# One written order for the whole program, and a written place for every temporary

## The chip, the cores and the metric

The kernel runs on one core of a Trainium2 chip. The metric is the device time of one execution in microseconds. Five engines matter: TensorE (PE, matrix products), VectorE (DVE), ScalarE (ACT), GpSimd (POOL), and SyncE (SP), which here only issues transfers between the chip's large memory (HBM) and the working memory (SBUF). Products are summed in PSUM, which has eight banks of 512 float32 per partition.

## What is computed

Attention in which each of 8 batches and 8 heads has 512 local tokens and 32 global ones, followed by a gated two-layer network over all 4608 tokens:

```python
s_g   = scale * q_g @ concat(k_g, k_l).T          # global queries see all keys
out_g = softmax(s_g) @ concat(v_g, v_l)
s_ll  = where(abs(i - j) <= 32, scale * q_l @ k_l.T, -1e9)
s_l   = concat(scale * q_l @ k_g.T, s_ll)         # local ones: a window and the globals
out_l = softmax(s_l) @ concat(v_g, v_l)

x   = concat(out_g, out_l) as (4608 tokens, 512)
xn  = x / sqrt(mean(x * x) + 1e-6) * rms_g
g   = xn @ w_gate                                 # 512 x 1536
h   = g * sigmoid(g) * (xn @ w_val)
out = h @ w_out                                   # 1536 x 512
```

## The kernel before

**Chunks.** The work is cut into nine chunks. Chunks 0 to 7 are the 512 local tokens of one batch each; chunk 8 is the 256 global tokens. While the network of chunk c runs on PE, the local attention of chunk c+1 and the global attention of some batch are threaded between its products. Attention is in float32. The network is in float16: every operand is split into a high and a low part, and each product is three products of parts. Chunks 0 and 1 do both layers plainly; chunk 2 does the first layer with seven block products in place of eight (tiles pq), chunks 3 to 7 do so for both layers (pq and pr), chunk 8 for the second.

**Steps.** The functions of the kernel are cut into named steps. In chunk 0: L, V and W load q and k, v, and a slice of weights; S (scores), M (mask and minimum), E (exponent), T (transposes), C (copies), A (products with v), R, X, Q, Z (division, sums of squares) are a unit of attention; m, s, k or l, g, q, p, e, a, d turn one weight slice into its two parts (a makes the high part on ACT, d the low one on DVE); N, D, U, H, Y are the norm; I are the first layer's products, B, b, h, c, r the gate on ACT and DVE (c a cast on ACT, r a subtraction on DVE, which give the two parts of h); O are the second layer's products; J, j, u, w build the sums of weights that the block products need and store them to HBM (wd, wa, wb). So r4 is r for slice 4, and M7.1 is M of unit 7, half 1. In chunks 1 to 8 a step has its chunk in front: P and O are products, R what follows a product, t the gate's tail, n the next chunk's norm, w the weight loads and folds due at that point, and a name with a slash (GT/1+1) is a step of an attention unit of a later chunk. From chunk 2 on the weights come back from HBM: `fetch` (L1339) loads a tile wt for two block products, `fetch_out` (L1348) a tile wu, all on SP's queue.

**Order.** All engines run under a manual schedule (L1903): each engine's queue holds its instructions in the order in which the program calls them, and every dependence between engines becomes a semaphore wait. For chunk 0 the order is the list ORDER, run step by step at L1904. For chunks 1 to 8 the steps are first recorded by `write` (L1910), cut where the engine changes, and then called in the order of one list per chunk at L2038:

```python
for c, plan in plans.items():
    for name in orders.get(c, plan):
        for call in plan.pop(name) if c in orders else plan[name]:
            call()
```

So all steps recorded under chunk c stand ahead of all those under chunk c+1, on every engine. L1929 in the profile is the helper that records, and so the line of nearly all instructions of chunks 1 to 8.

**Places.** A temporary takes the next buffer of its pool in rotation and waits until that buffer's earlier content is released. The pools in SBUF: wf 12 buffers of 4 KB a partition (weights, wt, wu, u, v, results), wo 7, h 6, st 6 of 4.5 KB, v 4, x 2, q 2, k 2, e 4, w 3, t 3, xh and xl 4 each, gpt 1. In PSUM: pa has four banks (attention), po two, pg one and pv one (products). Every PE product that begins a new sum, and every load, takes its buffer this way.

Of the kernel before, what the change touches and what calls it, by code (L numbers as in the profile page):

```python
# [39 lines left out]
ORDER = """  # L40

# [22 lines left out]


_ORDER_1 = """
w0.0 S/0+1.0 M1/0+1.0 E1/0+1.0 w2.0 M3/0+1.0 E3/0+1.0 P0.0 N2/0+1.0 P1.0 N3/0+1.0 M2/0+1.0 E2/0+1.0
N1/0+1.0 M0/0+1.0 w3.0 w5.0 E0/0+1.0 N0/0+1.0 F0/0+1.0 P4.0 w6.0 F3/0+1.0 P5.0 R5.0 R6.0 P8.0 P9.0
F1/0+1.0 D1/0+1.0 R9.0 R1.0 F2/0+1.0 D3/0+1.0 D3/0+1.1 R10.0 P6.0 P7.0 R7.0 D0/0+1.0 D2/0+1.0
D2/0+1.1 R2.0 T2/0+1.0 P10.0 P11.0 w8.0 w9.0 P12.0 P2.0 T3/0+1.0 P3.0 D0/0+1.1 T0/0+1.0 D1/0+1.1  # L70
T1/0+1.0 A/0+1.0 B/0+1.0 P14.0 w12.0 Y/0+1.0 R3.0 R4.0 R5.1 w14.0 R11.0 R12.0 w1.0 X/0+1.0 R8.0 R9.1
GL/1+1.0 w15.0 P18.0 P16.0 P17.0 X/0+1.1 P19.0 Y/0+1.1 R17.0 R18.0 R19.0 R20.0 P13.0 R13.0 P32.0
P33.0 w18.0 GS/1+1.0 GM/1+1.0 Y/0+1.2 R13.1 GN/1+1.0 P24.0 P25.0 R14.0 w45.0 w20.0 w21.0 GM/1+1.1
GN/1+1.1 GT/1+1.0 GN/1+1.2 GT/1+1.2 GT/1+1.1 GT/1+1.3 P15.0 R15.0 L/2+1.0 S/2+1.0 R33.0 R34.0
M0/2+1.0 M2/2+1.0 N0/2+1.0 w49.1 N1/2+1.0 M3/2+1.0 N3/2+1.0 w24.0 E3/2+1.0 F3/2+1.0 P20.0 w17.0
R21.1 P40.0 D3/2+1.0 R25.0 R26.0 N2/2+1.0 R16.0 E2/2+1.0 R17.1 P21.0 R21.0 P22.0 P23.0 D3/2+1.1
R22.0 R23.0 T3/2+1.0 w26.0 w27.0 R24.0 R25.1 P26.0 P27.0 R27.0 R28.0 V/2+1.0 E0/2+1.0 F0/2+1.0
M1/2+1.0 F2/2+1.0 P28.0 P29.0 P41.0 R41.0 R29.1 X/0+1.2 w30.0 Y/0+1.3 P34.0 w23.0 P35.0 P30.0
D0/2+1.0 D0/2+1.1 R29.0 P31.0 R35.0 w44.0 P42.0 R30.0 R31.0 GV/1+1.0 R42.0 E1/2+1.0 GA/1+1.0 P43.0
F1/2+1.0 D1/2+1.0 D1/2+1.1 T1/2+1.0 w32.0 w33.0 L/0+2.0 R36.0 R37.1 P36.0 GD/1+1.0 P38.0 P66.0 R43.0  # L80
R44.0 D2/2+1.0 T0/2+1.0 D2/2+1.1 T2/2+1.0 w38.0 P37.0 R37.0 R38.0 w47.0 R45.1 w40.0 A/2+1.0 B/2+1.0
Y/2+1.1 X/2+1.0 X/2+1.1 w41.0 R32.0 P39.0 X/2+1.2 P44.0 P45.0 Y/2+1.0 X/2+1.3 Y/2+1.2 Y/2+1.3 R39.0
R40.0 R45.0 R46.0 R41.1 S/0+2.0 N0/0+2.0 M3/0+2.0 n53.0 P46.0 P47.0 n53.1 w46.0 R47.0 E3/0+2.0 n55.0
n55.1 n55.2 N1/0+2.0 n55.3 V/0+2.0 N2/0+2.0 n55.4 w48.0 n55.5 R33.1 N3/0+2.0 M2/0+2.0 E2/0+2.0
F2/0+2.0 P48.0 P67.0 P68.0 P49.0 P50.0 n55.6 n55.7 n55.8 n55.9 n55.10 w48.1 w35.0 P69.0 P70.0 n55.11
n55.12 n55.13 P51.0 P52.0 n56.0 R48.0 R49.0 P71.0 D2/0+2.0 M1/0+2.0 w46.1 n57.0 GX/1+1.0 w29.0
M0/0+2.0 D2/0+2.1 E0/0+2.0 n57.1 n64.1 w42.0 w49.0 w51.0 n65.0 P53.0 F3/0+2.0 n63.2 R71.0 w11.0
R53.0 F0/0+2.0 P54.0 P55.0 w54.0 w43.0 E1/0+2.0 F1/0+2.0 n56.1 n58.0 n58.1 R71.1 n62.1 n59.0 n59.2
P56.0 P57.0 D0/0+2.0 D0/0+2.1 n61.1 w56.0 P58.0 P59.0 n59.1 n63.0 P60.0 P61.0 GX/1+1.1 T2/0+2.0
w57.0 R53.1 D3/0+2.0 D3/0+2.1 D1/0+2.0 D1/0+2.1 T1/0+2.0 n64.0 n63.1 n60.0 n61.0 n65.1 T3/0+2.0  # L90
P62.0 P63.0 w59.0 P64.0 P65.0 R65.0 T0/0+2.0 R59.0 n62.0 R65.1 R59.1 n66.0
"""
# [187 lines left out]
def attention_moe_kernel(  # L280
# [363 lines left out]
    def local_unit(c, hp):  # L644
# [1523 lines left out]
```

## Time and profile before

| | |
|---|---|
| three runs | 917.7, 919.26, 921.77 us (median 919.26) |
| profiled execution | span 922.7 us from first to last instruction; no other time of it is given |
| busy | PE 878.8 us (95%), DVE 724.5, ACT 556.3, POOL 273.2 |
| mean granted TensorE clock | 0.980 |
| read from HBM, written | 183.2 MB, 27.0 MB |
| DMA packets' share of the 16 engines' span | 69.5% for the hardware queue that carries the loads |

Busy time is the union of an engine's instructions. PE's matmuls are pipelined and their ends are modelled, so a busy PE may still lose short waits. The granted clock is a share of 2.4 GHz: 0.50 is the lower of the two levels, 1.2 GHz.

### The profile page before, as it was taken

The page shows a single profiled execution, that of the slowest core. Times are in us where ns is not written, and L with a number is a line of the kernel's source. Part 1 is how long each engine was busy: PE and PEld are TensorE (multiplying, and loading weights), DVE is VectorE, ACT ScalarE, POOL GpSimd, SP SyncE. Part 2 cuts the span into 40 slices and gives each one's busy share as a digit, 9 for nine tenths or more (in the row PEclk, how much of TensorE's full clock was granted, in tenths as well). Part 3 has the DMA queues.
Part 4 walks back from the last instruction along what each step waited for, and adds up shares of the span by engine and source line. Part 5 has one row for each costly group of instructions (what it writes and reads, how often), then busy time and mean ns, then how long its engine had stood idle before and what let it go on. Part 6 is the DMA issues. An engine that isn't in the chain of part 4 may idle for free.

```text
span 922.7 us, 27756 instructions
## 1 busy us (share of the span) xinstructions
PE 878.8 (95%) x11430; PEld 671.4 (73%) x11430; DVE 724.5 (79%) x1831; ACT 556.3 (60%) x1341; POOL 273.2 (30%) x244
## 2 busy tenths in 40 slices
PE   5699989999999999999999999898999999999998
PEld 4644445544547886588888888787888888888887
DVE  6899998868796887877987888587887897777554
ACT  6899995636452755457565767466575862456132
POOL 0000000032435776306440244122520454133311
PEclk9699989999999999999999999999999999999999
DMA  9983615495377869686677769667876666888665
GB/s 337 405 301 106 192 47 173 130 333 174 90 248 243 274 206 300 194 257 233 206 258 263 245 222 293 198 208 243 265 250 223 206 222 244 247 246 273 215 232 191
DMA packets 101006, 212.03 MB, mean 230 GB/s; under 512 B 8080, under 2 KB 34448, under 8 KB 100880
## 3 DMA queue, kind: packets, MB, share of 16 engines
q1 hardware_dynamic: 100448, 209.94, 69.5%
q8 instruction: 89, 1.46, 0.6%
q10 hardware_dynamic: 432, 0.33, 0.1%
q14 instruction: 37, 0.30, 0.1%
HBM read 183.24 MB, written 27.00 MB: 228 GB/s over the span
## 4 chain that ended last, share of the span: by engine, by line
PE 40%; DVE 5%; DMA 3%; ACT 3%; issue 2%; POOL 1%; DVEq 0%; ACTq 0%; POOLq 0%; SPq 0%
PE pq L1929 20%; PE pr L1929 14%; PE p L1929 3%; DMA wt<-wd 2%; ACT e L1929 1%; PE a L1929 1%; DVE v L1929 1%; DMA wu<-wb 1%; DVE s L1929 1%; DVE u L1929 1%; POOL hs L1929 1%; POOL hu L1929 1%; PE s L1929 1%; ACT s L1929 1%; DVE t L1929 1%
## 5 line engine op out<-in xcount | busy, mean ns | idle before, releaser
L1929 PEld LDWEIGHTS <-wt 128*128 128x128 f16 x3312 | 322.7, 98 | 56.9 <-issue 11.1
L1929 PE MATMUL pq<-xh,wt 128*128 128x256 f16 x1152 | 206.6, 274 | 6.8 <-DMA wt<-wd 2.5
L1929 PE MATMUL pq<-ht,wt 128*128 128x256 f16 x1296 | 158.0, 274 | 2.1 <-POOL ht L1929 1.2
L1929 PE MATMUL pq<-xl,wt 128*128 128x256 f16 x576 | 157.8, 274 | 0.1
L1929 ACT ACTIVATE e<-e,sm 128x128 f32<-128x128 f32 x288 | 104.2, 390 | 27.8 <-DVE sm L1929 27.8
L1929 POOL TENSOR_TENSOR hu<-v,hu 128x256 f16<-128x256 f32 (+1 forms) x60 | 56.5, 958 | 177.6 <-ACT hu L1929 155.1
L1929 PE MATMUL pr<-wu,hs 128*128 128x256 f16 x792 | 92.4, 273 | 0.3 <-DVE hs L1929 0.3
L1929 POOL TENSOR_TENSOR e<-e,sm 128x512 f32<-128x512 f32 x24 | 27.7, 1162 | 205.3 <-DVE sm L1929 205.3
L1929 PEld LDWEIGHTS <-hs 128*128 128x128 f16 x792 | 77.4, 98 | 9.7 <-DVE hs L1929 0.6
L1929 POOL TENSOR_TENSOR hs<-u,hs 128x512 f16<-128x512 f32 x50 | 60.5, 1228 | 65.6 <-ACT hs L1929 37.9
L1929 PE MATMUL pr<-wu,hu 128*128 128x256 f16 x594 | 70.8, 273 | 1.0 <-DMA wu<-wb 0.6
L1929 DVE TENSOR_TENSOR s<-pq,s 128x512 f32<-128x512 f32 x66 | 44.9, 685 | 29.9 <-PE pq L1929 14.1
L1929 ACT ACTIVATE t<-u,half_inv 128x512 f32<-128x512 f32 x72 | 49.6, 717 | 27.0 <-DVE u L1929 23.0
L1929 DVE SCALAR_TENSOR_TENSOR t<-t,u 128x512 f32<-128x512 f32 x72 | 54.0, 758 | 14.4 <-ACT t L1929 14.3
L1929 ACT COPY s<-pq 128x512 f32<-128x512 f32 x72 | 41.3, 580 | 38.3 <-DVE s L1929 18.2
L1929 PEld LDWEIGHTS <-hu 128*128 128x128 f16 x594 | 57.6, 98 | 8.6 <-DMA wu<-wb 0.9
L1929 DVE TENSOR_TENSOR v<-pq,s 128x512 f32<-128x512 f32 x72 | 49.0, 683 | 18.6 <-PE pq L1929 14.8
L1929 PE MATMUL po<-wo,h 128*128 128x512 f16 x288 | 63.4, 379 | 0.0
L1651 PE MATMUL p<-xh,wf 128*128 128x512 f16 x192 | 58.8, 379 | 3.1 <-DVE t L1763 1.2
L1929 PE MATMUL p<-xh,wf 128*128 128x512 f16 x192 | 59.8, 385 | 0.5 <-DVE t L1929 0.5
L1651 PEld LDWEIGHTS <-wf 128*128 128x128 f16 x288 | 27.7, 98 | 37.0 <-issue 3.1
L1929 PEld LDWEIGHTS <-wf 128*128 128x128 f16 x288 | 27.8, 99 | 34.6 <-issue 2.9
(380 smaller groups left out, 1704.7 us busy)
## 6 DMA issues: line engine op xcount, KB each, us to landing
wt<-wd SPq DMA_DIRECT2D x120, 512.0 KB, 5.3
wu<-wb SPq DMA_DIRECT2D x36, 512.0 KB, 5.3
wr<-in_w_in_dram SPq DMA_DIRECT2D x24, 512.0 KB, 8.7
wu<-wa SPq DMA_DIRECT2D x24, 512.0 KB, 4.7
k<-in_qkb_dram SPq DMA_DIRECT2D x24, 448.0 KB, 6.5
gkq<-in_gkq_dram SPq DMA_DIRECT2D x16, 576.0 KB, 7.1
wt<-wd SPq DMA_DIRECT2D x36, 256.0 KB, 4.2
v<-in_vb_dram SPq DMA_DIRECT2D x24, 352.0 KB, 5.6
```

The costliest lines, as they stand in the source:

```text
L1651: nc.tensor.matmul(ps[:, :n], rows[:, a, o : o + P], ch[z][k][:, :n], start=(k == 0 and i == 0), stop=(k == NK - 1 and i == 2),)
L1929: return lambda *a, **k: write(self.engine, lambda: call(*a, **k))
```

## The change

1. ORDER and the eight lists per chunk are replaced by one list ORDER of all 3365 pieces, each with its chunk in front; a list JOBS, equal to the old ORDER, only says in which order chunk 0's steps are recorded. The set of pieces is the same; chunk 0's steps are now cut where the engine changes, too, so that the parts of a step can stand apart, and pieces of neighbouring chunks may mix.
2. The pools are gone. SBUF holds 43 pages of 4 KB a partition and 8 wide ones of 4.5 KB, and the lists PAGES and BANKS give, in the order of recording, the page (with the quarter at which it begins) or the bank of each temporary. Temporaries under 1 KB a partition get memory of their own. All eight PSUM banks serve every use.
3. The transposed exponents of global attention are two tiles instead of one, and loads of gv and k are placed by their own size. A scratch space for DMA descriptors is set to 2048 bytes.

No instruction, shape, queue or engine changes. The core of the diff:

```diff
-ORDER = """
-
+JOBS = """
...
+NPAGE, NWIDE = 43, 8
+
+ORDER = """
+0:L0.0 0:S0.0 0:L1.0 0:L3.0 0:M0.0.0 0:M0.1.0 0:L2.0 0:W0.0 0:V0.0 0:S1.0 0:W1.0 0:M1.0.0 0:E0.0.0
...
+0:Y0.1.0 0:d1.0 0:q2.0 0:q3.0 0:S4.0 0:H0.0.0 0:d0.0 0:Y0.0.0 0:M4.0.0 0:U0.3.0 0:m5.0 0:H0.3.0
+0:U0.2.0 0:m4.0 0:I1.10.0 0:H0.2.0 0:k5.0 0:I0.00.0 0:Y0.3.0 0:s5.0 0:M4.1.0 0:Y0.2.0 0:k4.0 0:p2.0
...
+0:d12.0 0:S7.0 0:T5.0.0 0:C5.1.0 0:B11.0 0:O0.0.0 0:c6.0 0:M7.0.0 0:b11.0 0:C5.0.0 0:c4.0 0:A5.0
+0:a13.0 0:c7.0 0:R5.0 0:M7.1.0 0:a14.0 0:d13.0 0:Q4.0 0:O0.1.0 0:O0.2.0 0:M6.0.0 0:c5.0 0:a17.0
+0:a15.0 0:r6.0 0:r5.0 0:O1.1.0 0:V6.0 0:r7.0 0:O1.0.0 0:h11.0 0:E7.0.0 0:E7.1.0 0:O0.3.0 0:O1.3.0
...
+    page = [con.tile([P, 1024], F32, tag=f"page{i}", name=f"page{i}") for i in range(NPAGE)]
+    wide = [con.tile([P, 1152], F32, tag=f"wide{i}", name=f"wide{i}") for i in range(NWIDE)]
+    banks = [psum.tile([P, 512], F32, tag=f"bank{i}", name=f"bank{i}") for i in range(8)]
+    page_at, bank_at, smalls = iter(PAGES.split()), iter(BANKS.split()), [0]
+
+    def tile_of(shape, dt, name):
+        n = int(np.prod(shape[1:])) * (2 if dt in (F16, BF16) else 4) // 4
+        if n < 256:
+            smalls[0] += 1
+            tag = f"{name}_{smalls[0]}"
+            return con.tile(shape, dt, tag=tag, name=tag)
+        at = next(page_at)
+        if n > 1024:
+            t = wide[int(at[1:])][:, :n]
+        else:
+            of, i = (wide, at[1:-1]) if at[0] == "W" else (page, at[:-1])
+            q = ord(at[-1]) - ord("a")
+            t = of[int(i)][:, q * 256 : q * 256 + n]
...
+    def bank_of(name):
+        return banks[int(next(bank_at))]
...
     def fetch(c, g, i):
-        t = pool.tile([P, 2, 2, 2, HT], F16, tag="wf", bufs=NF, name=f"wt{c}_{g}{i}")
+        t = tile_of([P, 2, 2, 2, HT], F16, f"wt{c}_{g}{i}")
...
-    for c, plan in plans.items():
-        for name in orders.get(c, plan):
-            for call in plan.pop(name) if c in orders else plan[name]:
-                call()
-        assert c not in orders or not plan
+    for name in ORDER.split() or list(plan):
+        for call in plan.pop(name):
+            call()
+    assert not plan
```

In the old ORDER the same place of chunk 0 reads `a12 T5.0 d12 O0.0 O0.1 c8 Q4`, with c4 to c7, r4 to r7 and all M steps of units 4 to 7 ahead of it. In the old lists a load stands among the steps of its own chunk or the end of the chunk before; in the new one some stand a chunk earlier, as 3:w22.0 between steps of chunks 1 and 2.

## Rows read from the trace of the kernel before

**Rows 1.** The page, its first part: TensorE's busy time, its share of the span and its instructions; then PE's weight loads and the other engines.

```profile
PE 878.8 (95%) x11430; PEld 671.4 (73%) x11430; DVE 724.5 (79%) x1831; ACT 556.3 (60%) x1341; POOL 273.2 (30%) x244
```

**Rows 2.** Busy time by stage, core 0: the stretch (us from the start), its length, the busy time of PE, PE's weight loads, DVE, ACT and POOL with their counts, the granted share of TensorE's full clock, the mean busy share of the DMA engines, GB/s.

```profile
0.00:46.00 46.00, 29.16 (x611) 24.46 (x612) 34.42 (x151) 35.70 (x104) 0.20 (x4) 0.78 0.98 371
46.00:130.00 84.00, 76.37 (x712) 38.90 (x710) 81.23 (x193) 80.20 (x139) 0.00 (x0) 0.97 0.53 178
130.00:172.00 42.00, 42.00 (x496) 23.67 (x497) 35.69 (x84) 26.29 (x66) 0.00 (x0) 0.98 0.32 108
172.00:286.00 114.00, 110.67 (x1184) 55.09 (x1165) 90.80 (x241) 56.59 (x168) 40.83 (x32) 0.99 0.68 210
286.00:387.00 101.00, 100.16 (x1477) 74.12 (x1477) 80.31 (x195) 55.79 (x145) 61.81 (x45) 1.00 0.77 246
387.00:489.00 102.00, 98.49 (x1505) 85.78 (x1495) 81.59 (x208) 61.80 (x159) 38.04 (x35) 1.00 0.76 242
489.00:589.00 100.00, 95.92 (x1456) 84.00 (x1454) 80.08 (x207) 65.78 (x174) 31.53 (x30) 1.00 0.76 244
589.00:690.00 101.00, 98.15 (x1449) 84.88 (x1447) 77.15 (x201) 65.21 (x172) 32.23 (x29) 0.97 0.73 239
690.00:873.00 183.00, 182.37 (x2179) 160.21 (x2177) 139.29 (x293) 95.15 (x192) 61.29 (x58) 1.00 0.73 235
873.00:922.60 49.60, 45.55 (x416) 40.32 (x414) 23.91 (x65) 13.78 (x27) 7.25 (x13) 1.00 0.61 213
```

**Rows 3.** The list of waits, PE alone, from 0 to 172 us: who waited, for whom, us in total, times, the longest.

```profile
...
PE x00t L1110 <- DVE dg L1104: 6.3, 1, 6.3
...
PE t L732 <- ACT e L717: 4.1, 2, 3.0
...
```

**Rows 4.** The same list from 172 us to the end, whole. "issue" is time in which the engine waited for nothing that the profile shows.

```profile
PE pq L1929 <- DMA wt<-wd: 3.4, 4, 2.2
PE gt L1929 <- ACT ge L1929: 2.6, 2, 2.3
PE a L1929 <- issue: 2.4, 2, 2.2
PE pq L1929 <- DVE s L1929: 1.9, 4, 1.2
PE pq L1929 <- ACT u L1929: 1.5, 1, 1.5
PE pq L1929 <- POOL ht L1929: 1.2, 1, 1.2
PE pq L1929 <- DVE u L1929: 0.6, 1, 0.6
PE pr L1929 <- DMA wu<-wb: 0.6, 1, 0.6
PE p L1929 <- DVE t L1929: 0.5, 1, 0.5
PE pr L1929 <- DVE oo L1929: 0.4, 1, 0.4
PE pr L1929 <- DVE hs L1929: 0.3, 1, 0.3
```

**Rows 5.** Busy time by stretch again, for the three stretches after 172 us in which the granted clock was halved (columns as in rows 2).

```profile
210.50:213.90 3.40, 3.40 (x34) 1.43 (x39) 0.86 (x3) 1.54 (x4) 0.00 (x0) 0.50 0.57 160
589.40:592.80 3.40, 3.40 (x18) 2.36 (x17) 0.30 (x1) 1.32 (x4) 0.00 (x0) 0.50 0.99 266
626.90:630.30 3.40, 3.16 (x15) 2.24 (x16) 0.31 (x1) 3.35 (x14) 0.51 (x1) 0.50 0.99 295
```

**Rows 6.** The chain of waits, from 495 to 510 and from 615 to 650 us: start, length in us, what the chain ran through.

```profile
498.07 9.17 PE pq L1929 x84
...
623.53 3.56 DMA wt<-wd
...
639.43 4.27 DMA wt<-wd
```

**Rows 7.** The waits of SyncE's queue, which issues the transfers, over the whole run (columns as in rows 3), and the issue row of the page for the larger wt loads: count, KB each, median us from issue to landing.

```profile
SPq L1929 <- PE pq L1929: 142.3, 65, 9.9
...
SPq L1929 <- PE a L1929: 34.4, 4, 27.2
...
wt<-wd SPq DMA_DIRECT2D x120, 512.0 KB, 5.3
```

**Rows 8.** Groups of chunk 0. The first row is from the view of one line (L1794, chunk 0's output products): durations min/median/max in ns, first and last start in us. The others are groups from 0 to 172 us, with shapes kept apart: busy us, mean ns of one, idle time before.

```profile
L1794 PE MATMUL po<-wo,h x144: 379/379/634, 129.1 to 170.1; 128*128 128x512 f16 x144
...
L702 DVE CUSTOM_DVE_ANT_0 e<-s,mask 128x128 f32<-128x128 f32 x64 | 14.2, 291 | 8.6 <-PE s L688 8.6
...
L369 DVE TENSOR_TENSOR h<-t,h 128x512 f16<-128x512 f32 x12 | 8.1, 687 | 0.0
...
L485 ACT ACTIVATE wr<-wr 128x512 int16<-128x512 int16 x22 | 27.4, 1378 | 0.9 <-DVE w3t L474 0.9
...
L1774 ACT CAST h<-t 128x512 f16<-128x512 f32 x12 | 7.0, 610 | 0.3 <-DVE t L1766 0.3
```

**Rows 9.** The views of tile t on DVE and of tile h on POOL: durations min/median/max in ns, first and last start.

```profile
L1929 DVE SCALAR_TENSOR_TENSOR t<-t,u x72: 650/685/1625, 298.3 to 847.8; 128x512 f32<-128x512 f32 x72
...
L1929 POOL TENSOR_TENSOR h<-t,h x23: 1151/1164/2016, 193.6 to 360.9; 128x512 f16<-128x512 f32 x23
```

More of the change, by code (lines that the diff above doesn't have):

```diff
@@ L72 @@
[L72 to L77, printed above, removed]
@@ new lines @@
+8:R16.2 8:R8.4 8:R8.0 8:R16.4 8:P19.0 8:P30.0 8:P37.0 8:P16.0 8:P46.0 8:P32.0 8:R8.1 8:P33.0 7:R59.0
+8:R8.2 8:R8.3 8:R9.1 8:P17.0 8:w4.0 8:P31.0 8:R33.0 8:R10.0 8:R10.2 7:O36.0 8:P28.0 8:P29.0 7:O37.0
+8:R17.0 8:R18.4 7:O38.0 8:R10.3 8:R37.0 8:P22.0 8:R29.0 8:P47.0 8:R19.0 8:w42.0 8:R34.4 8:R18.0
+8:P34.0 8:R24.1 8:R30.0 8:R18.1 8:P24.0 8:O0.0 8:P23.0 8:P25.0 8:R23.0 8:R24.4 8:R24.0 8:R24.2
+8:R25.0 7:t45.2 8:R38.0 8:O3.0 8:R31.0 8:P38.0 8:R24.3 8:R16.3 8:R26.4 8:R17.1 8:R18.2 8:w32.0
+8:P35.0 8:R25.1 8:P39.0 8:R39.0 8:P26.0 8:R35.0 8:P27.0 8:R26.0 8:P42.0 8:R27.0 8:w44.0 8:P44.0
@@ new lines @@
+8:R10.1 8:O31.0 8:O24.0 8:O25.0 8:O26.0 8:O32.0 8:R34.1 8:R34.3 8:O27.0 8:O28.0 8:R56.2 7:R62.1
+8:O29.0 8:O33.0 8:O34.0 8:R62.0 8:R26.1 8:O35.0 8:R50.1 8:R65.0 8:R65.1 8:O36.0 8:O37.0 8:O38.0
+8:O39.0 8:O40.0 8:O41.0 8:R68.0 8:R68.1
+"""
+PAGES = """
+3a 0a 1a 0a 1a 0c 2a 0c 1c 7a 8a 22a 0a 5a 6a 5a 9a 10a 5c 0a 3c 4a 6a 20c 3c 2a 11a 7a 12a 13a 14a
+15a 3c 4a 16a 5a 1a 17a 6a 3c 18a 19a 15a 3c 23a 24a 9a 10a 16a 20c 14a 18c 7a 4a 20c 6a 15a 0a 3c
+20c 20b 20a 3d 0b 20a 21a 20d 21a 23a 9a 2a 8a 12a 13a 17a 28a 29a 26a 27a 30a 41a 24a 19a 22a 24c
@@ L679, in scores @@
             q, k = st["q"], st["k"]
-            st["sm"] = pool.tile([P, 3, 8], F32, tag="sm", bufs=SMB, name=f"sm{u}")
-            ps = st["ps"] = [bank(f"s{u}{h}", "pa") for h in range(2)]
+            st["sm"] = tile_of([P, 3, 8], F32, f"sm{u}")
+            ps = st["ps"] = [bank_of(f"s{u}{h}") for h in range(2)]
             for i in range(NT):
@@ L794, in load @@
             if w == 0:
-                late["mask"] = con.tile([P, 6 * P], F32, tag="mask", name="maskb")
+                late["mask"] = tile_of([P, 6 * P], F32, "maskb")
                 nc.sync.dma_start(late["mask"], maskb)
@@ L885, in scores @@
             st["et"] = [
-                pool.tile([P, 1088], F32, tag="k", name=f"et{u}{x}") for x in range(2)
+                tile_of([P, 1088], F32, f"et{u}{x}") for x in range(2)
             ]
@@ L909, in values @@
             if ms[0] == blocks[0]:
-                st["a"] = [attn_bank(f"a{u}{p}") for p in range(4)]
+                st["a"] = [bank_of(f"a{u}{p}") for p in range(4)]
             ps = st["a"]
@@ L931, in values, with taken @@
                         )
-        def take(z):
+        def taken(z):
             x = x_part(c, 2 * hp + z)
@@ L1362, in moe_pair @@
         st = {}
-        bank = {6: "po", 1: "pg", 5: "pv"}
+        own = (6, 1, 5)
         onto = {7: 6, 4: 6, 3: 5, 2: 1}
@@ L1374, in products @@
             hi, lo = ch["op"][p]
-            first = p in bank
+            first = p in own
             for j in range(2):
@@ L1903, in attention_moe_kernel @@
     ctx.enter_context(tc.manual_schedule(engines=every))
-    for name in ORDER.split():
-        job.pop(name)()
-    plans = {c: {} for c in range(1, NCH)}
-    at_work = [1, "", 0, ""]
+    plan = {}
+    at_work = [0, "", 0, ""]
     now = nc
@@ L1911, in write @@
         c, step, n, on = at_work
-        if on and (on != engine or step[0] in "Rtn"):
+        if on and (on != engine or c and step[0] in "Rtn"):
             n += 1
         at_work[2:] = n, engine
-        name = f"{step}.{n}"
-        assert name not in plans[c] or name == next(reversed(plans[c])), name
-        plans[c].setdefault(name, []).append(call)
+        name = f"{c}:{step}.{n}"
+        assert name not in plan or name == next(reversed(plan)), name
+        plan.setdefault(name, []).append(call)
     def doing(c, step):
@@ L1936, in attention_moe_kernel @@
     nc = Written
+    for name in JOBS.split():
+        doing(0, name)
+        job.pop(name)()
     stores = [steps[3] for f, steps in folds.items() if f"J{f}" not in job]
```

768 lines of the change are left out of this document (427 added, 341 removed), and 9 rows, old and new, of the table BANKS.

## Prediction

> **What bounds the kernel now.** I read the page's busy row first [rows 1]. TensorE (PE) is busy 878.8 of 922.7 us, so 43.9 us is all that any order of the same steps can take out of its idle time; VectorE (DVE) at 724.5 and ScalarE (ACT) at 556.3 look far from a limit, but these are means over stages that differ. So the second view is busy time by stage, cut where chunks begin [rows 2]. From 0 to 46 us PE is idle for 16.8 us; from 46 to 130 us for 7.6 us, while DVE is busy 81.2 of 84 and ACT 80.2 of 84: there both are the bound, and PE waits for what they make. From 130 to 172 us PE is never idle. After 172 us its idle time is 3.3, 0.8, 3.5, 4.1, 2.9, 0.6 and 4.1 us a stage, 19.3 in all, of which some 3.5 is the last result going out. The two chunks from 690 to 873 us lose 0.6 together: a chunk can run nearly without loss when its inputs come in time.
>
> The third view is the list of waits. Before 172 us PE waits longest for the norm of chunk 0 (dg, 6.3 us) and for attention exponents [rows 3]. After it [rows 4] I split the list by whom PE waits for: 4.0 us for transfers (wt 3.4, wu 0.6), and 11.4 us for DVE, ACT, POOL and an unnamed releaser: 2.6 + 2.4 + 1.9 + 1.5 + 1.2 + 0.6 + 0.5 + 0.4 + 0.3. The clock adds to these: three stretches of 3.4 us ran at 1.2 GHz, a granted clock of 0.50 [rows 5], each at or just after one of the three waits of 2.2 us or more of rows 4; work done there would take half as long at 2.4 GHz, so each costs 1.7 us. The fourth view is the chain of waits: at 623.5 us it leaves PE and runs through a load of wt for 3.56 us, at 639.4 us again for 4.27 [rows 6]. These loads were issued late because SyncE (SP) was held: it waited 142.3 us in 65 waits for PE to finish with a buffer that a load was to overwrite, and once 27.2 us for attention [rows 7]. A transfer of 512 KB takes 5.3 us to land [rows 7], and SP's queue is in order, so loads behind the held one wait too.
>
> **The change, part by part.** No arithmetic, transfer or instruction is dropped; every term is one of position. I compare positions thus: a 12-matmul P step costs PE 84 matmuls in 9.17 us, 109 ns each, 1.31 us [rows 6], and the work of an engine that stands ahead of a step in its queue is the sum of its steps in the order.
>
> *Chunk 0.* The point that sets PE's lateness is O0.0, chunk 0's first output product, which began at 129.1 us [rows 8] and behind which PE has 42 us without idle time. Its weights come last from d12 on DVE. Both orders put the same PE work ahead of O0.0. Ahead of d12 the new one leaves out r4 to r7, four 128x512 subtractions of 687 ns, and M7.1 and one M6 step, two times four mask operations of 291 ns with their reads hidden in part: 14.2 us over 64 is 0.22 us each, 1.8 for eight [rows 8]. 2.7 + 1.8 = 4.5 us less on the engine that is busy 97% of this stage. If ACT held O0.0 instead, the four casts c4 to c7 of 610 ns that go behind it make 2.4 at most [rows 8]. What is put off comes after, beside 42 us in which DVE is busy 35.7 and ACT 26.3 [rows 2]; 4.5 more leaves DVE 1.8 free: the cover is thin, and if it is gone, r4 to r7 make the O steps of chunk 0 late by what is over. The new order also puts k5 and parts of chunk 1's attention (S4, M4.0) ahead of chunk 0's first product: k5 is two ACT operations, 2.5 us [rows 8], which makes that product later at first. So the bounds are +2.5 and -7.6 (all idle time of this stage), and I take -4.5, from the rows of the engine that makes O0.0's last input.
>
> *Transfers.* I count, for each of the 222 loads of wt and wu, the PE work that the written order has between the load and the first P or O step that reads it. Before: half have less than 7.3 us and 83 less than the 5.3 us that a load takes. After: half have more than 34.8 us, and 25 less than 5.3. The two loads of rows 6 are those of 5:P23, which goes from 3.9 to 97 us, and of 5:P33, from 0 to 78; that of 8:O18, the wait on wu, goes from 6.2 to 144. So the 4.0 us of rows 4 and the slow stretch at 626.9 us go: -5.7. Bounds: 0, if pages hold SP as buffers did, and -20.5, if waits of other engines that began with a late load go too.
>
> *Steps of other engines.* I count in the same way PE steps after chunk 0 whose last input from DVE, ACT or POOL stands less than 0.7 us of PE work before them: 37 before, 57 after. The order is tighter here, not looser; against that, eight shared banks replace pools of 4, 2, 1 and 1, and PE steps move across chunks (2:P1 among steps of chunk 1, 7:O36 to 7:O41 among those of chunk 8), so more PE work is at hand when one step waits. The 11.4 us and the two other slow stretches, 3.4, make 14.8. At best all goes; at worst the 20 steps that are new each wait as in the third rival, +18.8. I take half of 14.8, -7.4, between the 690 to 873 us stage, which loses 0.3 a chunk, and 589 to 690 us, which loses 2.9 [rows 2].
>
> *Waits added.* A page that is written again makes the writer wait for its last reader. Where the writer is SP, all later loads stand behind it; the leads above are what absorbs this. *The end* (873 us on) keeps its last store: 0.
>
> Sum: 922.7 - 4.5 - 5.7 - 7.4 = 905.1 us on the profiled execution. No time of that execution beside its span is given; it is 0.4% above the median of the three runs, 919.26, so the forecast on the median is 919.26 x 905.1 / 922.7 = 902 us.
>
> **The rivals.**
> *A. All of it goes.* Stages from 172 us on run as that from 690 us, and the head gains its bound: 922.7 - 7.6 - 5.7 - 14.8 = 894.6, 891 on the median. For it: that two chunks already run so. Against it: 57 tight steps.
> *B. It doesn't do what it says.* SP is held by pages as it was by buffers, and what the order gains in one step the queues give back in the next: nothing changes after 172 us. 918.2 with the head's -4.5, 925.2 with its +2.5: 915 to 922 on the median. For it: 142.3 us of SP's waits come from memory being full, and the memory is as full as before. Against it: the loads of chunks 3 to 7 are written up to a chunk earlier, which only places that are free by then allow.
> *C. Tight steps wait: slower.* Place: the 57 PE steps with under 0.7 us ahead of them, 20 more than now. Price: DVE or POOL runs longer than the order counted on. A gate of 128x512 on DVE takes 685 ns in the median and 1625 at most, a POOL subtraction 1164 and 2016 [rows 9]: 0.94 us more where it happens. 20 x 0.94 = 18.8, so 922.7 - 4.5 - 5.7 + 18.8 = 931.3, 928 on the median. It decides from the 11th such wait on (10.2 / 0.94), and shows as slower than noise from the 16th. For it: two engines in order and an order that moves POOL's work against DVE's. Against it: of the 37 tight steps now, the waits of rows 4 are only 11.4 us over all steps.
> The Trainium skill (SBUF — State Buffer, "Who interferes with whom") has a cause for rival C: a VectorE operation with two SBUF inputs and a GpSimd operation exclude each other, and the later one waits for the whole of the other. The spread of rows 9 agrees in size: the excess of 0.94 us is less than one POOL operation of 1.16. By the rule an order that puts the two side by side pays on both engines; by the medians alone rival C would cost nothing.
>
> **How the numbers follow.** Forecast 0.55, A 0.17, B 0.12, C 0.13, and 0.03 for a gain between B and the forecast. Within 0.5% of 919.26 (914.7 to 923.9), about what a measurement can tell from no change, lies B; so faster 0.75, same 0.12, slower 0.13. The range runs from A, 891, less 2 for the spread of the runs (917.7 to 921.77), so 889, up to 922, the upper end of B; outside it lies C. The forecast's own range is 895 to 910.
>
> **What would show it.** O0.0 of chunk 0 begins near 125 us rather than 129.1. PE's waits on wt and wu after 172 us are under 1 us, SP's loads of wt land tens of us before use, and no stretch at 1.2 GHz after 172 us follows a transfer. Idle time of PE between 172 and 873 us falls from 15.2 to some 7 us. Wrong would be: waits of PE on DVE or POOL above 20 us there (C), SP's waits ahead of wt with PE waiting on them still (B), or an O0.0 later than 129 us, by which the head's term has the wrong sign.

## The result and the profile after

The changed kernel takes 928.14 us (median; 926.46 to 928.54) beside 919.26 before: ratio 1.0085, interval 1.0063 to 1.0108. Between the medians it is slower by 8.9 us, under 2%, and the interval does not reach 1; the forecast of 902 and its range 889 to 922 were wrong. The profiled execution took 926.46 us, 1.9 more than its span of 924.6.

The page's first part and the busy time by stage, cut where rows 2 are cut (columns as there):

```profile
PE 871.5 (94%) x11430; PEld 668.4 (72%) x11430; DVE 751.0 (81%) x1831; ACT 552.4 (60%) x1341; POOL 279.7 (30%) x244
```

```profile
46.00:130.00 84.00, 77.34 (x759) 40.20 (x741) 81.79 (x195) 81.93 (x144) 0.00 (x0) 1.00 0.70 244
...
172.00:286.00 114.00, 112.72 (x1322) 60.59 (x1321) 96.47 (x248) 59.10 (x171) 43.65 (x35) 1.00 0.72 223
286.00:387.00 101.00, 96.79 (x1387) 70.94 (x1386) 82.63 (x187) 51.78 (x140) 58.73 (x44) 1.00 0.76 241
387.00:489.00 102.00, 97.61 (x1485) 84.31 (x1485) 87.82 (x216) 63.11 (x161) 39.14 (x33) 1.00 0.82 274
489.00:589.00 100.00, 97.33 (x1395) 84.76 (x1393) 84.73 (x203) 63.18 (x162) 34.20 (x30) 1.00 0.72 241
589.00:690.00 101.00, 95.15 (x1412) 83.45 (x1410) 79.42 (x199) 65.67 (x182) 30.84 (x27) 0.98 0.69 235
690.00:873.00 183.00, 179.28 (x2279) 156.74 (x2277) 145.06 (x291) 95.17 (x195) 64.33 (x58) 1.00 0.68 236
```

Against [rows 1], DVE is busy 26.5 us longer with the same 1831 instructions: they have become longer. Against [rows 2], two stages lose less of PE's time: that from 172 us (1.3 us, not 3.3) and that from 489 us (2.7, not 4.1). The others lose more: 286 to 387 us 4.2 where it lost 0.8, 387 to 489 us 4.4 (3.5), 589 to 690 us 5.9 (2.9), 690 to 873 us 3.7 (0.6). From 172 to 873 us PE is idle for 22.1 us; it was 15.2 before, and the forecast had some 7.

PE's list of waits from 172 us on, to be held against [rows 4]:

```profile
PE bank L2059 <- DVE page L2059: 9.7, 17, 1.3
PE bank L2059 <- issue: 6.4, 5, 3.8
PE bank L2059 <- ACT page L2059: 2.7, 2, 2.6
PE bank L2059 <- DVE gsm L2059: 1.6, 1, 1.6
PE bank L2059 <- DMA wide<-wa: 0.6, 1, 0.6
PE bank L2059 <- POOL page L2059: 0.4, 2, 0.2
PE bank L2059 <- ACT wide L2059: 0.2, 1, 0.2
```

Transfers have gone from 4.0 to 0.6, as meant. But DVE has gone from 3.7 us in 8 waits to 11.3 in 18, and time that nothing shown ends ("issue") from 2.4 to 6.4.

Which of DVE's instructions became longer is plain in a view of tile "page" on DVE (durations min/median/max in ns, first and last start):

```profile
L2059 DVE TENSOR_TENSOR page<-page,page x169: 280/673/1671, 70.8 to 915.7; 128x256 f32<-128x256 f32 x72, 128x512 f16<-128x512 f32 x45, 128x512 f32<-128x512 f32 x18, 128x128 f32<-128x128 f32 x12
L2059 DVE TENSOR_TENSOR page<-bank,page x156: 645/684/693, 283.1 to 849.0; 128x512 f32<-128x512 f32 x156
```

With one input from PSUM (bank) and one from SBUF (page), 156 instructions lie between 645 and 693 ns: no spread. The first row mixes shapes, but with both inputs from SBUF some take over twice as long as their shape does elsewhere. Which ones can be counted in the trace. VectorE's two-input operations (TENSOR_TENSOR and SCALAR_TENSOR_TENSOR) with both inputs of 512 columns in SBUF take, where no GpSimd operation overlaps them (209), 0.64 to 0.78 us; of the 78 that a GpSimd operation overlaps, 46 take over 0.85, up to 2.19. Of those with one input in PSUM that a GpSimd operation overlaps (89), none takes over 0.75. In the kernel before 55 are overlapped, not 78, and 36 of them take over 0.85. How it looks in place, in the timeline (start, us, engine, operation; in brackets PE's idle time and who ended it):

```profile
462.73 4.13 POOL L2059 TENSOR_TENSOR page<-page,page 128x512 f16<-128x512 f32 x3 [4.18 <-DMA page<-wb]
...
464.34 1.50 DVE L2059 TENSOR_TENSOR page<-page,page 128x512 f16<-128x512 f32 x1
...
465.90 0.83 PE L2059 MATMUL bank<-wide,page 128*128 128x256 f16 x6 [0.67 <-DVE page L2059]
```

A subtraction that takes 0.68 us elsewhere takes 1.50 while GpSimd subtracts, and PE waits 0.67 us for it.

Two measures are used from here on, both worked out from a trace. **Lengthening**: for each kind and shape of VectorE's instructions what each takes over the 20th percentile of its kind, summed where it is over 0.15 us. **Lateness** of a step: its start on PE less the PE work that the kernel's order puts ahead of it, each step at its time in the first trace of before; where it grows, PE lost time. Its level depends on how a step's time is taken, so only its growth and the difference between two columns are read; taking it otherwise moves these differences by at most 0.8 us.

### The profile page after: what moved, and what is told of

It is laid out like the page before. It is cut to its first block, busy times and chain, and to the rows that moved or that the text cites. A ratio compares the mean times of both kernels' runs of the same rounds, so it can differ in the third digit from the quotient of the medians.

```text
span 924.6 us, 27862 instructions
## 1 busy us (share of the span) xinstructions
PE 871.5 (94%) x11430; PEld 668.4 (72%) x11430; DVE 751.0 (81%) x1831; ACT 552.4 (60%) x1341; POOL 279.7 (30%) x244
## 3 DMA queue, kind: packets, MB, share of 16 engines
q8 instruction: 89, 1.46, 0.6%
## 5 line engine op out<-in xcount | busy, mean ns | idle before, releaser
L2059 PE MATMUL bank<-page,page 128*128 128x256 f16 (+4 forms) x7944 | 748.5, 285 | 35.9 <-DVE page L2059 14.8
L2059 PEld LDWEIGHTS <-page 128*128 128x128 f16 (+1 forms) x5406 | 519.2, 98 | 185.3 <-issue 20.8
L2059 POOL TENSOR_TENSOR page<-page,page 128x512 f16<-128x512 f32 (+5 forms) x180 | 209.6, 1183 | 372.6 <-ACT page L2059 308.5
L2059 ACT CAST page<-page 128x512 f16<-128x512 f32 (+1 forms) x156 | 122.5, 801 | 104.7 <-DVE page L2059 90.7
L2059 DVE TENSOR_TENSOR page<-bank,page 128x512 f32<-128x512 f32 x156 | 105.2, 683 | 49.7 <-PE bank L2059 33.2
L2059 ACT COPY page<-bank 128x512 f32<-128x512 f32 (+3 forms) x163 | 84.1, 539 | 102.4 <-PE bank L2059 87.0
L2059 ACT ACTIVATE page<-page,sm 128x128 f32<-128x128 f32 x344 | 126.7, 390 | 30.3 <-DVE sm L2059 30.2
L2059 DVE TENSOR_TENSOR page<-page,page 128x256 f32<-128x256 f32 (+5 forms) x169 | 112.4, 676 | 10.2 <-ACT page L2059 8.0
L2059 DVE TENSOR_TENSOR page<-page 128x256 f32<-128x256 f32 (+3 forms) x121 | 76.6, 639 | 2.5 <-PE bank L2059 0.5
L2059 ACT ACTIVATE page<-page 128x512 f32<-128x512 f32 (+2 forms) x85 | 70.8, 905 | 8.5 <-DVE page L2059 7.4
L2059 DVE CUSTOM_DVE_ANT_0 page<-bank,page 128x128 f32<-128x128 f32 x252 | 57.8, 283 | 11.8 <-PE bank L2059 11.7
L2059 DVE SCALAR_TENSOR_TENSOR page<-page,page 128x512 f32<-128x512 f32 x64 | 50.2, 802 | 10.3 <-ACT page L2059 10.2
```

The source lines that it names most:

```text
L2059: return lambda *a, **k: write(self.engine, lambda: call(*a, **k))
```

## The experiments

Theory 1: VectorE and GpSimd exclude each other when both read SBUF, and the new order puts more of that side by side. Theory 2: the order's leads are short, whatever the lengths. Theory 3: waits for pages and banks to come free.

**Second traces.** Both kernels once more, unchanged.

> The kernel before once more, for a second trace on this chip: 917 to 922 us. The forecast was made from one trace whose span, 922.7, lies above the times of the timed runs. If that trace was an unlucky draw, this one shows less idle time of PE after 172 us than the 15.4 us of the first and fewer than three half-clock stretches there; the forecast's terms for transfers (5.7) and for stalls (14.8) were then too large. If not, the same within 2 us.

> The changed kernel once more, for a second trace: 926 to 929 us. Theory 1: VectorE's lengthening is again above 65 us, and the stalls of PE after 172 us come at the same steps as in the first trace (1:P54, 2:P34, 3:P3, 7:P37). If the stalls fall on other steps, the loss is chance and not the order.

918.85 us (span 916.7) and 927.42 (925.6). Before: lengthening 41.9 us in 75 instructions, after 72.0 in 108 (first traces 41.7 and 72.6): it belongs to the kernel, not to chance; the stalls come at the same steps. Idle time of PE after 172 us is 15.9 us before, as in the first trace. But of the three half-clock stretches of [rows 5] only the one near 210 us is there again, and the span is 6 us shorter: the forecast's sum of 922.7 began from a long draw. The lateness of these two traces, in us:

| step | before | after |
|---|---|---|
| O0.0 of chunk 0 (start 128.0, 126.4) | 34.5 | 32.9 |
| first step of chunk 2 | 40.6 | 36.8 |
| of chunk 3 | 43.0 | 41.9 |
| of chunk 4 | 50.2 | 49.4 |
| of chunk 5 | 55.8 | 54.1 |
| last P step of chunk 6 | 61.6 | 66.9 |
| the last | 62.1 | 71.0 |

The new order is 3.8 us ahead when chunk 2 begins and 8.9 behind at the end, which is the difference of the medians. Most of the loss is in chunk 5 and after.

**GpSimd's reads taken away.** For the low halves of the gated products GpSimd subtracts 16 columns only and then fills the tile twice, which reads no SBUF (shortened):

```diff
-        sub("P", dst, a, b)
+        gpsimd.tensor_tensor(dst[:, :16], a[:, :16], b[:, :16], subtract)
+        gpsimd.memset(dst, 0.0)
+        gpsimd.memset(dst, 0.0)
```

> In the changed kernel, GpSimd no longer subtracts for the low halves of the gated products (tiles h, hu and hs of chunks 2 to 7): it subtracts 16 columns only, after the same wait, and then writes the tile twice with zeros, which reads no SBUF. So these low halves are zero: the products lose their second half of precision. Order, places, PE work and transfers are those of the changed kernel. Theory 1 (VectorE and GpSimd exclude each other when both read SBUF, and the new order puts more of them side by side): the lengthening of VectorE (sum over its operations of what is above the 20th percentile of their form, where it is over 150 ns; 72.6 us in the changed kernel, 41.7 in the one before) falls below 40 us, and the time falls by 9 us or more, to 919 or less. Theory 2 (the order's leads are short, whatever the lengths): the lengthening falls, but the time falls by less than 4 us, to 924 or more. Theory 3 (waits for pages and banks to come free): the time stays within 2 us of 928.1.

> The same edit in the kernel before: GpSimd subtracts 16 columns of the low halves of the gated products and writes zeros for the rest. Theory 1: the lengthening falls from 41.7 us to some 25, and the time falls by less than half of what the changed kernel loses by this edit, so that the two kernels come within 4 us of each other. Theory 2: both fall by the same amount within 3 us, and 6 to 9 us stay between them. Theory 3: 917 to 921, no change.

919.04 us (ratio to before 0.9999, 0.9975 to 1.0022) and 920.02 (1.0003, 0.9984 to 1.0022). The changed kernel loses 9.1 us by the edit, the one before none, and the difference between them is gone. Lengthening falls from 72 to 35 us in the changed kernel and from 42 to 26 in the one before; GpSimd is no shorter (busy 292.5 us, 279.7 without the edit), so it is not that its results come sooner. The same subtraction as above, in the trace of after_memset:

```profile
460.19 0.52 POOL L551 MEMSET page<- 128x512 f16 x1
460.66 0.69 DVE L2070 TENSOR_TENSOR page<-page,page 128x512 f16<-128x512 f32 x1
460.68 0.74 POOL L549 TENSOR_TENSOR page<-page,page 128x16 f16<-128x16 f32 x1
461.48 0.52 POOL L550 MEMSET page<- 128x512 f16 x1
...
462.55 0.22 POOL L549 TENSOR_TENSOR page<-page,page 128x16 f16<-128x16 f32 x1
```

VectorE's takes 0.69 us; the 16-column subtraction, 0.22 for the next tile, starts just behind it and takes 0.74: now GpSimd is the one that waits. Another such subtraction has fills (MEMSET), which only write, beside nearly all of it:

```profile
852.22 0.52 POOL L550 MEMSET page<- 128x512 f16 x1
852.39 0.65 DVE L2070 TENSOR_TENSOR page<-page,page 128x512 f16<-128x512 f32 x1
...
852.80 0.53 POOL L551 MEMSET page<- 128x512 f16 x1
```

It takes 0.65 us, and of the 13 operations with two SBUF inputs of 512 columns that fills alone overlap for 0.3 us or more, none takes over 0.75. Theories 2 and 3 fall by the times they gave: order, places and waits are those of the changed kernel, and 9.1 us are back. The rule of the Trainium skill that rival C drew on (SBUF — State Buffer, "Who interferes with whom") has a VectorE operation with two SBUF inputs contend with a GpSimd one that reads SBUF, and not with one that only writes it. The traces agree on both: 1.50 us beside the subtraction, 0.65 beside the fills.

**Shorter holds.** GpSimd does the same subtractions in two operations over half of the columns; in after_hall its other operations after chunk 0 too, the softmax products excepted (shortened):

```diff
-        gpsimd.tensor_tensor(dst, a, b, subtract)
+        for half in (left, right):
+            gpsimd.tensor_tensor(dst[half], a[half], b[half], subtract)
```

> In the changed kernel GpSimd subtracts the low halves of the gated products in two operations over half of the columns each, in place of one over 512. Nothing else changes. Theory 1 (exclusion: VectorE waits until GpSimd's operation is over): an operation then holds VectorE for some 0.7 us at most rather than 1.2, the lengthening falls from 72 us to between 45 and 62, and the time to between 920 and 926. Theory 2 (short leads whatever the lengths): GpSimd's results come later by the fixed cost of the second operation, the time is 928 or more.

> The same edit in the kernel before: lengthening falls from 42 us to 30 to 38, and the time moves by less than 2 us, 917.5 to 921.5, by theory 1 as by theory 2: its stalls after 172 us lie behind loads, ScalarE and PE's instructions more than behind lengthened operations.

> In the changed kernel every GpSimd operation after chunk 0 but the softmax products is done as two over half of the columns (after_halves did so for the gated products alone). Theory 1 (exclusion): the lengthening falls below the 58 us of after_halves, to 45 to 54, the stalls of 1 to 2.7 us in chunks 1 and 2 that stand behind folds on VectorE become shorter, and the time is 917 to 921.5. If smaller pieces only add fixed costs: 922 to 925.

921.91 us (1.0038, 1.0011 to 1.0066), 923.59 (1.0048, 1.0021 to 1.0076), and 920.23 (1.0011, 0.9984 to 1.0039). Lengthening in the changed kernel: 72, then 58, then 54. No work is left out, and 6 to 8 of the 8.9 us are back. In the kernel before the edit costs 4.3 us, against both theories as I had priced them. One place of it is in the chains of waits, here of the second trace of before and of before_halves (start, length in us):

```profile
615.16 2.60 POOL hu L1929 x3
617.76 2.43 POOL hs L1929 x2
620.19 0.02 issue
620.20 3.48 DMA wt<-wd
```

```profile
615.85 3.30 POOL hu L385 x6
619.16 2.53 POOL hs L385 x4
621.69 0.02 issue
621.71 3.57 DMA wt<-wd
```

The load of wt waits for a buffer until GpSimd is done, and PE for the load: there the second operations add 0.8 us. This is the late load of [rows 6], from which the new order is free. In the whole list, PE's waits on wt are 7.0 us in before_halves and 3.3 in before_rep; what else makes up the 4.3 us is open.

**The subtractions on VectorE.** `units("P")`, `splits("P")` and `low(j, on="P")` become "V"; in after_Vs the splits alone.

> In the changed kernel the subtractions for the low halves of the gated products (h, hu, hs of chunks 2 to 7) are done by VectorE, at the same places of the order. That adds 87 operations of 128x512 at 0.69 us and 36 shorter ones to VectorE, some 75 us on top of 751, and takes 155 us off GpSimd. If exclusion is what made the changed kernel slow (theory 1), lengthening falls below 40 us and gives back some 35; VectorE is then busy some 790 us, and the time depends on what is left of its leads: 915 to 925. If the leads in the order alone decide (theory 2), VectorE's 40 us more make it slower: 930 to 945.

> In the changed kernel only the subtractions for hs (chunks 3 to 7, 50 of 128x512) move from GpSimd to VectorE, 34 us more there. Theory 1: the lengthening falls by a third or more, from 72 to under 50 us, and the time falls to 918 to 925. Theory 2: 928 to 938.

> The kernel before with all low halves of the gated products subtracted by VectorE. Its lengthening is 41.7 us, of which the edit without reads took 16; VectorE gains 75 us of work. Theory 1: there is little to win by less exclusion here, so the added work shows: 920 to 935, and the changed kernel gains more from the same edit than this one. Theory 2: both lose the same within 3 us.

955.11 us (1.0392, 1.0365 to 1.0419), 943.47 (1.0272, 1.0242 to 1.0302) and 965.77 (1.0505, 1.0463 to 1.0546): worse than any theory had it. Lengthening falls, but less than expected in the changed kernel (from 72 to 47 and 62; in the one before from 42 to 33). The sum of VectorE's durations grows by 51 us in after_V and 67 in before_V, and PE's waits on DVE in after_V reach 30.8 us. VectorE has no room for it on the path: its busy share of 81% hides that PE waits for it step by step. That the changed kernel loses 27 us and the one before 46.5 speaks against equal losses (theory 2), but the remedy is none.

**GpSimd's other reads too.** Of nearly all its work after chunk 0 GpSimd does 16 columns and fills the rest with a constant, so the output's values mean nothing. One place of it:

```diff
-        nc.gpsimd.tensor_tensor(sq, sq, chunks[c]["sq"], ALU.add)
+        nc.gpsimd.special(sq, sq, chunks[c]["sq"], ALU.add, 1.0)  # 16 columns and two fills
```

> In the changed kernel nearly all of GpSimd's work after chunk 0 (low halves, sums of squares, the sums of the folded output weights, two sums of partial products; not the softmax products) is 16 columns of the operation and two fills with a constant, so the values of the output mean nothing. It follows after_memset, where 6.7 us of PE's stalls were left behind VectorE's folds of chunks 1 and 2, lengthened by GpSimd's other work. Theory 1: these go too, and the time falls from 919 to between 910 and 915. If what is left is the order's short leads: 918 to 920.

> The same edit in the kernel before. Theory 1: 917 to 921, since no long stall of it has a lengthened operation in its chain. The difference to after_memall is then what the written order is worth when nothing excludes anything: the forecast said 17 us; 5 to 9 are left by the lateness of PE in the traces without reads.

910.87 us (0.9901, 0.9874 to 0.9927) and 918.62 (0.9985, 0.9967 to 1.0004). With lengthening at 8 and 7 us the written order is worth 7.75 us. After minus before, in us of time, and the difference of their lengthening:

| | time after - before | lengthening after - before |
|---|---|---|
| as they are | +8.9 | 30 |
| halves | -1.7 | 20 |
| reads of the gated products away | -1.0 | 10 |
| nearly all reads away | -7.75 | 1 |

The two middle rows do not follow the last column: the halves also made the kernel before 4.3 us slower. That the written order is worth something by itself rests on the last row.

PE's waits in after_memall from 172 to 873 us are these two rows alone:

```profile
PE bank L2070 <- issue: 8.8, 7, 3.8
PE bank L2070 <- DVE page L2070: 1.2, 2, 0.9
```

No transfer and hardly a computed value is late any more: so far the order does what the forecast said. What is left is "issue".

**The gaps that nothing ends.** First, four loads moved away from the longest one:

```diff
 5:w52.0
+6:w13.0 7:w3.0 5:w59.0 5:w57.0
```

(they stood between 5:w46.0 and 5:w53.0)

> In the changed kernel four loads of wt (first read by PE at 693, 704, 725 and 807 us) stand in SP's queue behind a load that goes out near 668 us instead of going out between 638.6 and 644.3 us, where the DMA engines are busy 0.96 to 1.02. Nothing else moves. PE stands still for 3.8 us from 645.7 us in step 5:B/2 with nothing to wait for but its own instructions. Theory 1 (the packet with PE's instructions, which landed at 648.0, stood behind the bulk loads): that gap falls below 2 us, the half-clock stretch behind it goes, and the time falls by 2.5 to 6 us, to 922 to 925.6. Theory 2 (short matmuls run through their instructions faster than these can come, whatever the loads): the gap stays above 3 us and the time within 2 us of 928.1.

928.62 us (1.0101, 1.0072 to 1.013), gap 3.64 us: as theory 2 of that run has it. Its timeline of PE, and the DMA queues from 649 to 650 us (queue, packets, MB, share of 16 engines), show what the gap is:

```profile
645.34 2.34 PE L2059 MATMUL bank<-wide,page 32*64 32x256 f32 x151
651.33 0.32 PE L2059 MATMUL bank<-wide,page 32*64 32x32 f32 x9 [3.64 <-issue]
```

```profile
q8 instruction: 1, 0.02, 5.8%
q1 hardware_dynamic: 1, 0.00, 0.1%
```

151 matmuls, each with its weight load, pass in 2.34 us; then PE stands until 1.4 us after one packet of 16 KB on the queue of instructions (649.04 to 649.96). The packet begins 1.4 us after PE has stopped. The loads were not wholly out of its way: the DMA engines are busy to 0.89 until PE stops and to 0.35 in the 1.3 us behind that; only from 649 us on does nothing else move. But in the changed kernel, where they are busy to 1.01 and 0.95 in the first 1.3 us of the gap and after, it is not much longer (3.8 us, 4.5 in the second trace), and in all three traces it stands behind the same matmul, the 151st. Queue 8 moves 1.46 MB in a run of the changed kernel,

```profile
q8 instruction: 89, 1.46, 0.6%
```

64 bytes for each of PE's 11,430 matmuls and 11,430 weight loads: by this it is PE's. So I read the gap thus: PE has used up its instructions faster than the next came. Moving the four loads doesn't help; that earlier loads hold the packet up a little isn't excluded. The Trainium skill (Runtime: NRT & Kernel Launch, "Instruction fetch mechanics") gives blocks of the same size and calls the cost of crossing one mostly hidden; by this reading it isn't here, behind short matmuls.

Second, two runs of short matmuls are moved apart:

```diff
-5:P37.0 5:R34.1 5:P36.0 5:GD/1+1.0 5:t31.1 5:A/2+1.0 5:R36.0 5:B/2+1.0
+5:P37.0 5:R34.1 5:A/2+1.0 5:P36.0 5:GD/1+1.0 5:t31.1 5:R36.0 5:B/2+1.0
```

and 5:S/0+2.0 goes behind 5:O15.0. A/2 takes the bank that GD still has to read, so chunk 5's global rows are made from other values; the work of each engine is the same.

> In the changed kernel two steps of short matmuls in chunk 5 change their place in the order: A/2 (80 matmuls) goes ahead of P36, so that A/2 and B/2 no longer follow each other on PE, and S/0 of the next pair (128) goes behind O15. The loads are those of the changed kernel. Theory 2 of after_loads (a run of short matmuls uses up PE's instructions faster than the next 16 KB of them come): the gaps of 3.8 and 1.1 us there fall below 1.5 and 1 us, the half-clock stretch behind goes, and the time falls by 2 to 6 us to 922 to 926. If the gap belongs to a place in the instruction stream whatever the step: it stays near 3.8 us, the time 927 to 929.

926.8 us (1.0098, 1.0067 to 1.0128). The gap of 3.8 us becomes 2.2, that of 1.1 behind S/0 goes, and "issue" falls from 6.4 to 3.6: the gaps go with the runs of short matmuls. It is less than was expected: the half-clock stretch stays (from 651.6 us), and of 2.8 us saved the time shows 1.3, within what such runs spread. One reason stands in the list of waits: where S/0 stood, PE now waits for GpSimd.

```profile
PE bank L2059 <- POOL page L2059: 1.2, 1, 1.2
```

**Together.**

> after_hall and after_issue together. If both act and on different stalls, the gains add: 928.1 less 7 to 10 and less 2 to 6, so 912 to 919, level with or faster than the kernel before (919.3). If after_issue does nothing, the time of after_hall.

> The halves of after_hall, and in chunk 5 the step A/2 ahead of P37 and P36 (with the step GD, which reads the bank that A/2 takes, ahead of it), S/0 of the next pair behind O15. In after_issue and after_both A/2 stood ahead of GD, so that the outputs of chunk 5's global rows were made from another step's scores. If runs of short matmuls outrun PE's instructions, two P steps between A/2 and B/2 give more than the one of after_issue, where 2.2 us of the 3.8 were left: gap below 1.5 us, and the time 913 to 918, faster than the kernel before (919.0) by over 0.2%. If the gap stays at 2.2 us: 917 to 919, level.

> after_memall (GpSimd's operations after chunk 0, softmax products apart, as 16 columns and two fills; the values mean nothing) with the order of after_both2. In after_memall PE loses 13 us to its order in chunk 5 and 6 to 7 in all other chunks from 2 on; of the 13, 3.8 and 3.0 are gaps that no semaphore ends and 3.4 two half-clock stretches behind them. If these two are what is left between the order and its forecast, the time falls from 910.9 to between 902 and 907, the forecast's 902 to 905. If the gaps only move elsewhere: 909 to 912.

918.16 us (0.9997, 0.9975 to 1.0019), 918.27 (0.999, 0.9967 to 1.0012) and 908.45 (0.988, 0.9846 to 0.9914). As far as the spread of the runs lets one see, the gains add. In after_both A/2 stands ahead of GD as in after_issue; after_both2 puts GD ahead of it again. after_both2, which leaves no work out, is 9.9 us below the changed kernel, by GpSimd's operations in halves and three steps (GD, A/2, S/0) in other places, and level with the kernel before: it isn't shown to be faster, which was expected. Its gap without a releaser at B/2 is gone, but A/2, moved further ahead, now waits 3.3 us for DVE, and a half-clock stretch of 6.8 us follows. Without nearly all reads and with the gaps broken up the order is worth 10.2 us (918.62 of before_memall less 908.45), of a forecast 17: between the two outcomes that had been named, 902 to 907 and 909 to 912.

**The head.** M7.1 and M6.0 go from ahead of d12 to behind O0.0 in the list of the kernel before, which keeps its pools.

```diff
-... q15 M7.1 A4 K0 K1 X4 E5.0 K2 S6 M6.0 a12 T5.0 d12 O0.0 O0.1 ...
+... q15 A4 K0 K1 X4 E5.0 K2 S6 a12 T5.0 d12 O0.0 M7.1 M6.0 O0.1 ...
```

> The kernel before with one piece of the change's head: the masks M7.1 and M6.0 of chunk 1's attention (eight operations of 291 ns on VectorE) stand behind O0.0 of chunk 0 instead of ahead of d12. The forecast put 0.22 us on each, 1.8 in all, of its 4.5 for the head. By that, O0.0 begins 1 to 2 us earlier than 128.0 and the time falls by 0 to 2 us, to 917.3 to 919.5. If ScalarE or another step holds O0.0, it begins at 128 as before.

926.32 us (1.0082, 1.0046 to 1.0117), slower by 7; O0.0 starts at 132.3 instead of 128.0. PE's waits from 100 to 135 us have a new first row:

```profile
PE s L686 <- DVE sm L700: 3.3, 1, 3.3
```

A score step (s), ahead of O0.0 in PE's queue, now waits 3.3 us for the masks to empty its bank, and a half-clock stretch of 10.2 us follows. Saving DVE work ahead of d12 was not the whole of it: with four attention banks the two steps, moved alone, hold up S. In the changed kernel, with eight shared banks, they do stand behind O0.0, and it starts at 125.9 us. The other part of the head (r4 to r7) was not measured by itself.

## Why the prediction was wrong

- **What bounds the kernel.** Right that PE's idle time is what can be won and that it splits into late loads and late values. Wrong in taking one trace for the kernel: two of the three half-clock stretches, counted as 1.7 us each of gain, were not in the second trace.
- **Chunk 0, -4.5.** Right in sign; in size too large. O0.0 starts at 125.9 and 126.4 us after 129.1 and 128.0, so -3.2 and -1.6; by the start of chunk 2 it is -3.8 in the second traces. The working (0.22 us for each mask operation) is not borne out alone, as before_rm shows.
- **Transfers, -5.7.** Right: waits on loads fall from 4.0 to 0.6 us. The slow stretch behind one of them was chance, so the term is some -3.4. Rival B falls: PE hardly waits for a load any more. One reason given for the late loads was incomplete: in the chain of before_rep the load near 620 us is held by GpSimd (hu, hs), not by PE.
- **Steps of other engines, -7.4.** This is the step that failed. I took half of 14.8 as gain, between -14.8 and +18.8. The waits that it counted, 11.4 us, came out as 21.0: DVE 11.3, "issue" 6.4, ACT 2.9, POOL 0.4. The length of the same instructions was treated as a constant, while VectorE's busy time grew by 26.5 us. Taking away GpSimd's reads of the gated products alone gives 9.1 us back, and nearly all of its reads 17.3.
- **Rival C** had the cause and, by its 928, the time; its chance of 0.13 was too low. The counts (57 tight steps against 37, and the row of 1625 ns beside 685) were there, and "the waits now are only 11.4 us" was a poor reason against it: these rows tell of the old neighbours of each instruction, not of the new ones. Its size is right in part by luck. It wanted over 20 us of waits on DVE and POOL; there are 11.7, in 20 waits, and the rest of the loss is another term.
- **The term that nobody had**: PE's instructions. Before, "issue" stood in rows 4 with 2.4 us and was counted among stalls that the order would cover. It rose to 6.4, with a half-clock stretch behind the longest, and in after_memall it is nearly all that is left.

## What to carry to other kernels

An order written from a table of durations holds only while the durations do: before moving VectorE work beside GpSimd work, look at min, median and max of each kind of instruction, and take a long maximum on those with two SBUF inputs (and none on those with one in PSUM) as a price that moves with the order. GpSimd's operations cut in halves hold the other engine for less time: here that gave the changed kernel 6.2 us back, but cost the one before 4.3, so it has to be measured; moving their work to VectorE was far worse in both. Take two traces before counting half-clock stretches as gain.

## What was not expected of the hardware

By the reading above PE can run out of instructions: in a run of 160 short matmuls it stops behind the 151st, 2.34 us after the first, and stands for up to 4.5 us, until 1.3 to 1.5 us after a packet of 16 KB. A half-clock stretch follows (columns as in rows 2; the changed kernel, first trace, right behind its gap of 3.8 us):

```profile
650.20:653.60 3.40, 3.40 (x18) 2.37 (x17) 2.03 (x4) 3.37 (x6) 1.27 (x2) 0.50 0.06 19
```

The exclusion works in both directions. In after_memset a GpSimd subtraction of 16 columns takes 0.21 to 0.22 us when it begins beside no VectorE operation (35 of them); of the 40 that begin beside one with two longer SBUF inputs, half take over 0.46, up to 0.74.
